# Moving the low-part subtractions of the mixing stages from GpSimd to VectorE

## The chip, the cores and the metric

One core of one Trainium2 chip runs the whole program. The metric is the device time of one execution in microseconds (us), given as the median of three runs. The engines are named as in the profile: PE is TensorE (PEld its weight loads), DVE is VectorE, ACT is ScalarE, POOL is GpSimd and SP issues transfers.

## The reference

Three layers follow each other. The first is windowed attention over q, k and v (4 batches, 8 heads, 576 tokens, 64 channels a head). The second is a mixture of four attention experts with two of them gated per token. The third is the one that the change touches; `x` is the result of the second layer, four batches of 576 tokens by 512 channels:

```python
theta = x @ w_theta
zr, zi = x * np.cos(theta), x * np.sin(theta)
y = np.einsum('ts,bsd->btd', w_tok_r, zr) + np.einsum('ts,bsd->btd', w_tok_i, zi)
u = x + y
return u + np.maximum(u @ w_ch, 0.0)
```

## The kernel before

**Split operands.** A matrix product in near-full precision is made of three products of a reduced format (`mm3`, L108 to L111): an operand is split into a high part (a cast by ACT) and a low part, the original minus the high part, and the kernel multiplies high by high, high by low and low by high. The helper `split` (L101) issues the ACT cast (L103) and then the subtraction (L106) on the engine that its last argument names. The subtraction needs the cast's result, so it waits for ACT.

**The stages at the end of the program.** The third layer is worked off by batch `b` and by half `dh` of the channels (256 columns each). `theta(b, dh)` (L649) goes through tiles of 128 tokens, 256 columns each; for every tile PE makes the angles and transposes x, ACT and DVE reduce the angle and take sine and cosine (L671 to L676), and DVE multiplies them with x (L679). That is the block z, 128x512, cosine half and sine half together. For the first three pairs (b, dh) the block is split straight away (L683). For the later ones two tiles are taken together by `sums_of` (L617): DVE makes four sums and differences of the blocks (L628, L629, L633, L637), and the blocks X, W, Y and V are split, each with an ACT cast and a subtraction. Tiles of the last 64 tokens of two batches are handled together (L687 to L694); their subtraction stands on GpSimd before and after the change.

**Mixing.** For the first three pairs `mix(b, dh)` (L697) multiplies the z blocks with the token weights; the later ones use `mix7` (L757), which makes a two by two block product with seven products instead of eight and needs X, W, Y and V for it. Both add the product to x2T on DVE (L717, L785), and four of the sums per `mix7` are also made on POOL (L791). The result, x plus y, is split in pieces of 128x288 as the input `cu` of the channel mixing (L718, L787). `channel(b)` (L833) multiplies with w_ch, DVE adds the rectified product (L843) and SP writes it out (L845).

**Work beside it.** `load_ch` (L878) turns the 64-bit channel weights into split parts in eight steps; each has a shift (L139) and a bit merge (L145) on DVE, an integer add on POOL (L147), a cast, and a subtraction on DVE (L153). `halves` (L720) makes combinations of the token weights for `mix7`: an add on POOL (L733), one on DVE (L734), four differences on DVE (L736 to L739) and splits.

**The order of the work.** `merge` (L50) interleaves the generators of a stage by cost numbers written by hand; the calls that matter here are L955 to L979. Then a scheduler orders each engine's instructions by that priority in its own simulated time, engine by engine, and places the semaphores. Every engine runs its instructions in that order, so an instruction that waits holds back everything behind it on its engine. `tc.issue_after(ins)` puts the instructions in its block that run on the engine of `ins` behind it. In `halves` the block at L732 stands under two of these: one names `d`, the DVE product of a z block (L679), and the other names `p`, the subtraction that `split` or `sums_of` returned for it:

```python
d, p = mark[((0, 1, 3), (1, 0, 0), (1, 0, 2), (1, 0, 3))[j]]
with tc.issue_after(p.ins), tc.issue_after(d.ins):
    nc.gpsimd.tensor_add(out=flat[:, 0], in0=f32(wkh[2 * j]), in1=f32(wkl[2 * j]))
    nc.vector.tensor_add(out=flat[:, 1], in0=f32(wkh[2 * j + 1]), in1=f32(wkl[2 * j + 1]))
```

Of the kernel before, what the change touches and what calls it, by code (L numbers as in the profile page):

```python
# [42 lines left out]
def f32(ap):  # L43
    return ap.bitcast(F32)
# [21 lines left out]
def kernel(ctx, tc, qT, kT, vw, consts, w_in, w_o, w_th, w_tk, w_ch, outT):  # L66
    nc = tc.nc
# [24 lines left out]
    def bank(shape, tag, name):  # L92
        return ps.tile(shape, F32, tag=tag, bufs=BANKS[tag], name=name)
# [7 lines left out]
    def split(dst_h, dst_l, src, eng_h, eng_l):  # L101
        if eng_h is nc.scalar:
            cast[0] = nc.scalar.copy(out=dst_h, in_=src)  # L103
        else:
            eng_h.tensor_copy(out=dst_h, in_=src)
        return eng_l.tensor_sub(out=dst_l, in0=src, in1=f32(dst_h))  # L106

    def mm3(out, wh, wl, xh, xl, first, last):  # L108
        nc.tensor.matmul(out, wh, xh, start=first, stop=False)  # L109
        nc.tensor.matmul(out, wh, xl, start=False, stop=False)  # L110
        nc.tensor.matmul(out, wl, xh, start=False, stop=last)  # L111
# [435 lines left out]
    Z, UH, XT, GT, mark, W4 = {}, {}, {}, {}, {}, 4 * P  # L547

    def hl_set(tags, name):
        t = [bp.tile([P, S], F32R, tag=tag, bufs=3 if tag in ("oh", "ol") else 1, name=f"{name}{i}")  # L550
             for i, tag in enumerate(tags)]
        return t[0::2], t[1::2]
# [27 lines left out]
    def load_o(n):  # L580
        while line and n:
            b, dh, i = line.pop(0)
            o = bp.tile([P, 4, P], F32R, tag=f"{'QK'[len(ring) % 4 // 2]}{'SA'[len(ring) % 4 // 2]}{len(ring) % 2}", name=f"or{b}{dh}{i}")
            nc.sync.dma_start(f32(o), od[b][:, :, i * P : i * P + P])
            ring.append(o)
            n -= 1
# [22 lines left out]
    def slot(tag, shape, name):  # L609
        pool, bufs = homes[tag]  # L610
        return pool.tile(shape, F32R, tag=tag, bufs=bufs, name=name)

    def operand(name):
        tag = free.pop(0)
        return tag, slot(tag, [P, 2, 2, 2, P], name)

    def sums_of(b, dh, i, ang):  # L617
        A11, A21, A12, A22 = (ang[:, :, q, k] for q in range(2) for k in range(2))
        if i == 1:
            Z[b, dh] = {}  # L620
        ops = Z[b, dh]
        n = f"{b}{dh}{i}"
        st = (rp if i == 1 else kp).tile([P, 2, 2, P], F32, tag="z", name=f"s{n}")
        s1, s2 = st[:, :, 0], st[:, :, 1]
        x = operand(f"X{n}")
        nc.scalar.copy(out=x[1][:, 0], in_=ang[:, :, :, 0])
        p = nc.gpsimd.tensor_sub(out=x[1][:, 1], in0=ang[:, :, :, 0], in1=f32(x[1][:, 0]))
        nc.vector.tensor_add(out=s1, in0=A21, in1=A22)  # L628
        nc.vector.tensor_sub(out=s2, in0=s1, in1=A11)  # L629
        w = operand(f"W{n}")  # L630
        nc.scalar.copy(out=w[1][:, 0], in_=st)
        nc.gpsimd.tensor_sub(out=w[1][:, 1], in0=st, in1=f32(w[1][:, 0]))
        nc.vector.tensor_sub(out=A21, in0=A11, in1=A21)  # L633
        y = operand(f"Y{n}")
        nc.scalar.copy(out=y[1][:, 0], in_=ang[:, :, :, 1])
        nc.gpsimd.tensor_sub(out=y[1][:, 1], in0=ang[:, :, :, 1], in1=f32(y[1][:, 0]))
        nc.vector.tensor_sub(out=A12, in0=A12, in1=s2)  # L637
        if i == 1:
            tag = free.pop(0)
            ops["V"] = tag, slot(tag, [P, 2, 4, P], f"V{n}")  # L640
        v = ops["V"][1]
        sl = slice(i - 1, i + 1)
        nc.scalar.copy(out=v[:, 0, sl], in_=A12)
        nc.vector.tensor_sub(out=v[:, 1, sl], in0=A12, in1=f32(v[:, 0, sl]))
        for k, t in zip("XWY", (x, w, y)):
            ops[k, i // 2] = t
        return p

    def theta(b, dh):  # L649
        x2 = x2T[b]  # L650
        dsl = slice(dh * HW, dh * HW + HW)
        for i in range(4 if b % 2 else 5):
            n = f"{b}{dh}{i}"
            if i < 4:
                tok = slice(i * P, i * P + P)
                o = ring[8 * b + 4 * dh + i]
                load_o(1)
                x32, ow = (lambda c: x2[:, c, tok]), [o[:, k] for k in range(4)]
            else:
                xt, xo = XT[0]  # L660
                x32, ow = (lambda c: xt[:, c]), [xo[:, k] for k in range(4)]
            th = bank([P, HW], "bs", f"th{n}")
            for c in range(2):
                mm3(th, ow[2 * c], ow[2 * c + 1], GT[c][0][:, dsl], GT[c][1][:, dsl], c == 0, c == 1)
            xk = bank([P, HW], "tb", f"xk{n}")
            for c in range(2):
                nc.tensor.transpose(xk[:, c * P : (c + 1) * P], x32(2 * dh + c), ident)
            if i % 2 == 0:
                ang = bp.tile([P, 2, 2, HW], F32, tag="bms", bufs=2, name=f"ang{n}")
            rn, sn = ang[:, i % 2, 0], ang[:, i % 2, 1]  # L670
            nc.scalar.activation(out=rn, in_=th, func=AF.Identity, bias=magic)  # L671
            nc.vector.scalar_tensor_tensor(out=rn, in0=rn, scalar=-MAGIC, in1=th,
                                           op0=ALU.add, op1=ALU.subtract)
            nc.scalar.activation(out=sn, in_=rn, func=AF.Sin, scale=-TWO_PI)
            nc.scalar.activation(out=rn, in_=rn, func=AF.Abs)
            nc.scalar.activation(out=rn, in_=rn, func=AF.Sin, bias=halfpi, scale=-TWO_PI)  # L676
            if i < 4:
                both = ang[:, i % 2]
                d = nc.vector.tensor_mul(out=both, in0=xk.unsqueeze(1).to_broadcast([P, 2, HW]), in1=both)  # L679
                if 2 * b + dh < 3:  # L680
                    zt = slot(first[8 * b + 4 * dh + i], [P, 2, 2, HW], f"z{n}")
                    Z[b, dh, i] = zt
                    mark[b, dh, i] = d, split(zt[:, :, 0], zt[:, :, 1], both, nc.scalar, nc.gpsimd)  # L683
                elif i % 2:
                    mark[b, dh, i] = d, sums_of(b, dh, i, ang.rearrange("p j q (k n) -> p j q k n", k=2))
            else:
                for k in range(2):  # L687
                    zt = kp.tile([P, 1, 2, HW], F32R, tag=f"zt{k}{dh}", name=f"z{n}{k}")
                    Z[b + k, dh, i] = zt
                    z = (rp, kp)[k].tile([P, HW], F32, tag="z", name=f"zf{n}{k}")  # L690
                    r = slice(64 * k, 64 * k + 64)
                    for q, tr in enumerate((rn, sn)):
                        nc.vector.tensor_mul(out=z[64 * q : 64 * q + 64], in0=xk[r], in1=tr[r])
                    split(zt[:, 0, 0], zt[:, 0, 1], z, nc.scalar, nc.gpsimd)  # L694
            yield 1.5

    def mix(b, dh):  # L697
        x2 = x2T[b]
        if dh == 0:
            UH[b] = hl_set(utags, f"cu{b}")  # L700
        uh, ul = UH[b]
        y = [bank([P, 288], tag, f"y{b}{dh}{k}") for k, tag in enumerate(("g", "g", "as", "ta"))]
        for c in range(9):
            zt = Z[b, dh, c // 2]
            q = c % 2 if c < 8 else 0
            for k in range(4):
                n, mm = divmod(k, 2)
                sl = slice(288 * n, 288 * n + 288)
                ms = slice(mm * P, mm * P + P)
                mm3(y[k], zt[:, q, 0, ms], zt[:, q, 1, ms], wkh[c][:, sl], wkl[c][:, sl],  # L710
                    c == 0, c == 8)
            yield 1.45
        for k in range(4):
            n, mm = divmod(k, 2)
            m = 2 * dh + mm
            sl = slice(288 * n, 288 * n + 288)
            nc.vector.tensor_add(out=x2[:, m, sl], in0=y[k], in1=x2[:, m, sl])  # L717
            split(uh[m][:, sl], ul[m][:, sl], x2[:, m, sl], nc.scalar, nc.gpsimd)  # L718

    def halves():  # L720
        f1 = rp.tile([P, 4, 288], F32, tag="x2b", name="t1")
# [35 lines left out]
    def mix7(b, dh):  # L757
        x2 = x2T[b]
        if dh == 0:
            UH[b] = hl_set(utags, f"cu{b}")  # L760
        uh, ul = UH[b]
# [22 lines left out]
        def add(m, sl, g, ready=False):  # L784
            nc.vector.tensor_add(out=x2[:, m, sl], in0=g, in1=x2[:, m, sl])  # L785
            if ready:
                split(uh[m][:, sl], ul[m][:, sl], x2[:, m, sl], nc.scalar, nc.gpsimd)  # L787

        def spread(u, *homes):
            for m, sl in homes:  # L790
# [3 lines left out]
        y = lambda k, tag: bank([P, 288], tag, f"y{k}{n}")  # L794
# [13 lines left out]
        g = y("d", "ta")  # L808
        yield from seven(g, lambda j: left(j, "W", 0), lambda j: TT[1, j], True, True)
        add(m1, s1, g)  # L810
        add(m2, s1, g)
        g = y("e", "g")
# [224 lines left out]
```

## Time and profile before

| what | us |
| --- | --- |
| median of three runs | 502.05 |
| lowest and highest | 500.07, 503.29 |
| the profiled execution, its time | 501.43 |
| the profiled execution, its span | 499.6 |

The span is the stretch between the first and the last instruction that the profile shows; the time has 1.8 us more around it. The profiled execution is 0.6 us below the median. All places in the trace are given in us from the start of the span: the third layer's mixing begins at about 300, `mix7` begins at about 374, the last channel mixing ends at about 496. "Idle before" in a group of instructions is the time that its engine stood still just before them, with what ended that wait.

### The profile page before, as it was taken

The page shows a single profiled execution, that of the slowest core. Times are in us where ns is not written, and L with a number is a line of the kernel's source. Part 1 is how long each engine was busy: PE and PEld are TensorE (multiplying, and loading weights), DVE is VectorE, ACT ScalarE, POOL GpSimd, SP SyncE. Part 2 cuts the span into 40 slices and gives each one's busy share as a digit, 9 for nine tenths or more (in the row PEclk, how much of TensorE's full clock was granted, in tenths as well). Part 3 has the DMA queues.
Part 4 walks back from the last instruction along what each step waited for, and adds up shares of the span by engine and source line. Part 5 has one row for each costly group of instructions (what it writes and reads, how often), then busy time and mean ns, then how long its engine had stood idle before and what let it go on. Part 6 is the DMA issues. An engine that isn't in the chain of part 4 may idle for free.

```text
span 499.6 us, 12071 instructions
## 1 busy us (share of the span) xinstructions
PE 475.9 (95%) x4128; PEld 446.2 (89%) x4128; DVE 381.6 (76%) x1283; ACT 342.2 (68%) x1054; POOL 319.3 (64%) x411
## 2 busy tenths in 40 slices
PE   7899899999999997999989999899999989999997
PEld 5689788999999897998878799899999989999997
DVE  6868989867779659877898969977668948893843
ACT  7948688867878756868787897876167717752620
POOL 6758789674776770323694556679558925891770
PEclk9999999999999999999999999999999999999999
DMA  8564253431316234112235953231362044202002
GB/s 272 182 227 134 67 179 108 139 100 49 125 60 198 78 97 147 33 38 92 88 120 168 349 176 144 71 78 43 100 175 65 23 143 131 65 22 96 2 0 96
DMA packets 45614, 55.92 MB, mean 112 GB/s; under 512 B 6641, under 2 KB 34289, under 8 KB 45553
## 3 DMA queue, kind: packets, MB, share of 16 engines
q1 hardware_dynamic: 44688, 52.46, 33.6%
q10 hardware_dynamic: 864, 2.69, 1.4%
q8 instruction: 33, 0.54, 0.4%
q14 instruction: 29, 0.23, 0.2%
HBM read 43.34 MB, written 11.80 MB: 110 GB/s over the span
## 4 chain that ended last, share of the span: by engine, by line
PE 52%; DVE 18%; ACT 15%; POOL 6%; issue 5%; DMA 3%; SPq 0%; DVEq 0%; ACTq 0%; POOLq 0%
PE as L297 3%; PE bpt L504 3%; ACT ams L313 2%; PE c L109 2%; PE c L110 2%; PE c L111 2%; PE apt L325 2%; PE qk L109 2%; PE bs L472 2%; PE qk L110 2%; PE ao L168 2%; PE qk L111 2%; PE bs L474 2%; PE o L522 2%; DMA wst<-in_dram 1%
## 5 line engine op out<-in xcount | busy, mean ns | idle before, releaser
L320 POOL TENSOR_TENSOR ams<-ams,arc 128x384 f32<-128x384 f32 x48 | 40.4, 845 | 34.4 <-DVE arc L319 14.3
L313 ACT ACTIVATE ams<-ams,anm 128x128 f32<-128x128 f32 x144 | 56.5, 396 | 4.0 <-DVE anm L305 2.9
L481 ACT ACTIVATE bms<-bms,bnm 64x64 f32<-64x64 f32 (+4 forms) x80 | 44.9, 562 | 13.1 <-DVE bnm L476 13.1
L297 PE MATMUL as<-kt,QD 128*128 128x128 f32 x288 | 41.2, 281 | 2.7 <-DVE anm L305 2.5
L297 PEld LDWEIGHTS as<-kt,QD 128*128 128x128 f32 x288 | 36.0, 192 | 6.2 <-DVE anm L305 2.9
L96 POOL TENSOR_SCALAR QD<-qt 64x576 f32<-64x576 f32 x24 | 30.6, 1274 | 11.7 <-DMA qt<-in_dram 4.6
L305 DVE CUSTOM_DVE_ANT_0 ams<-as,cst 128x128 f32<-128x128 f32 x144 | 34.1, 283 | 4.9 <-PE as L297 2.7
L476 DVE CUSTOM_DVE_ANT_0 bms<-bs,mb 64x64 f32<-64x64 f32 (+4 forms) x80 | 32.5, 422 | 5.4 <-PE bs L474 3.7
L106 POOL TENSOR_TENSOR cu<-x2T,cu 128x288 fp32r<-128x288 f32 x32 | 28.3, 901 | 9.9 <-ACT cu L103 9.8
L493 POOL TENSOR_SCALAR bpd<-bms,bsm,gw 128x64 f32<-128x64 f32 (+1 forms) x46 | 20.4, 445 | 20.2 <-DVE bsm L486 8.7
L109 PE MATMUL y<-wkh,z 128*128 128x288 f32 x108 | 32.1, 303 | 0.8 <-DVE x2T L717 0.8
L472 PE MATMUL bs<-KA,QS 128*128 128x288 f32 (+4 forms) x96 | 31.0, 331 | 1.1 <-DVE bnm L476 1.0
L110 PE MATMUL y<-wkl,z 128*128 128x288 f32 x108 | 31.9, 297 | 0.0
L679 DVE TENSOR_TENSOR ang<-xk,ang 128x512 f32<-128x512 f32 x32 | 21.6, 686 | 13.0 <-ACT ang L676 10.8
L111 PE MATMUL y<-wkh,z 128*128 128x288 f32 x108 | 30.9, 297 | 0.0
L671 ACT ACTIVATE ang<-th,magic 128x256 f32<-128x256 f32 x36 | 16.7, 470 | 18.8 <-PE th L111 17.7
L791 POOL TENSOR_TENSOR x2T<-x2T,u 128x288 f32<-128x288 f32 x20 | 16.9, 855 | 19.7 <-DVE u L802 18.1
L504 PE MATMUL bpt<-cst,bms 128*128 128x128 f32 x160 | 27.5, 276 | 1.5 <-ACT oh L103 1.5
L493 POOL TENSOR_SCALAR bms<-bms,bsm,gw 128x384 f32<-128x384 f32 (+3 forms) x38 | 24.7, 650 | 5.9 <-ACT wtuk L138 3.8
L474 PE MATMUL bs<-KL,QS 128*128 128x288 f32 (+4 forms) x96 | 28.4, 302 | 0.0
L313 ACT ACTIVATION_READ_ACCUMULATOR ams<-ams,anm 128x1 f32 x144 | 27.6, 192 | 0.0
L843 DVE SCALAR_TENSOR_TENSOR x2T<-c,x2T 128x288 f32<-128x288 f32 x32 | 13.8, 453 | 16.9 <-PE c L111 16.8
(337 smaller groups left out, 2051.7 us busy)
## 6 DMA issues: line engine op xcount, KB each, us to landing
vt<-in_dram SPq DMA_DIRECT2D x48, 192.0 KB, 2.9
or<-od SPq DMA_DIRECT2D x32, 256.0 KB, 3.3
kt<-in_dram SPq DMA_DIRECT2D x15, 320.0 KB, 3.1
qt<-in_dram SPq DMA_DIRECT2D x16, 288.0 KB, 3.6
out_dram<-x2T SPq DMA_DIRECT2D x32, 144.0 KB, 1.8
w64k<-in_dram SPq DMA_DIRECT2D x5, 576.0 KB, 4.2
od<-oh SPq DMA_DIRECT2D x8, 288.0 KB, 2.7
od<-ol SPq DMA_DIRECT2D x8, 288.0 KB, 2.8
```

Of the source, the lines that this page charges most:

```text
L109: nc.tensor.matmul(out, wh, xh, start=first, stop=False)
L110: nc.tensor.matmul(out, wh, xl, start=False, stop=False)
L111: nc.tensor.matmul(out, wl, xh, start=False, stop=last)
L297: nc.tensor.matmul(s[:, i, :], qd[:, blk], kt[:, 64 * blk : 64 * blk + 128], start=True, stop=True)
L305: nc.vector.tensor_tensor_reduce(out=ms[:, i, :], in0=s[:, i, :], in1=ma0 if (g == 0 and i == 0) else ma1, scale=-0.125, scalar=3.0e38, op ...
L313: nc.scalar.activation(out=ms[:, i, :], in_=ms[:, i, :], func=AF.Exp, bias=nm[:, i : i + 1], scale=-1.0, accum_out=sm[:, i, 0:1],)
L320: nc.gpsimd.tensor_mul(out=ms, in0=ms, in1=rc.unsqueeze(2).to_broadcast([P, 3, P]))
L472: nc.tensor.matmul(s[:, : z - a], qs[:, q0 : q0 + P], ka[:, a:z], start=True, stop=False)
L474: nc.tensor.matmul(s[:, : z - a], qs[:, q0 : q0 + P], KL[e][:, a:z], start=False, stop=True)
L481: ex = nc.scalar.activation(out=ms[:m, :w], in_=ms[:m, :w], func=AF.Exp, bias=nm[:m, ci : ci + 1], scale=-1.0, accum_out=ss[:m, i, 0:1])
L493: eng.tensor_scalar(out=dst, in0=src, scalar1=sm[:m, i : i + 1], scalar2=gw[:m, t, 2 * ep + i : 2 * ep + i + 1], op0=ALU.mult, op1=ALU.mult)
L504: nc.tensor.transpose(pt[:, jj, i, :], pn[:, i, P * j : P * j + P], ident)
```

## The change

Six subtractions get another engine: the low parts of X, W and Y in `sums_of`, those of the z blocks that `theta` splits directly, and those of the channel mixing's input in `mix` and `mix7`. Nothing else is edited. No operand, tile, transfer or matmul differs.

```diff
         x = operand(f"X{n}")
         nc.scalar.copy(out=x[1][:, 0], in_=ang[:, :, :, 0])
-        p = nc.gpsimd.tensor_sub(out=x[1][:, 1], in0=ang[:, :, :, 0], in1=f32(x[1][:, 0]))
+        p = nc.vector.tensor_sub(out=x[1][:, 1], in0=ang[:, :, :, 0], in1=f32(x[1][:, 0]))
         nc.vector.tensor_add(out=s1, in0=A21, in1=A22)
         nc.vector.tensor_sub(out=s2, in0=s1, in1=A11)
         w = operand(f"W{n}")
         nc.scalar.copy(out=w[1][:, 0], in_=st)
-        nc.gpsimd.tensor_sub(out=w[1][:, 1], in0=st, in1=f32(w[1][:, 0]))
+        nc.vector.tensor_sub(out=w[1][:, 1], in0=st, in1=f32(w[1][:, 0]))
         nc.vector.tensor_sub(out=A21, in0=A11, in1=A21)
         y = operand(f"Y{n}")
         nc.scalar.copy(out=y[1][:, 0], in_=ang[:, :, :, 1])
-        nc.gpsimd.tensor_sub(out=y[1][:, 1], in0=ang[:, :, :, 1], in1=f32(y[1][:, 0]))
+        nc.vector.tensor_sub(out=y[1][:, 1], in0=ang[:, :, :, 1], in1=f32(y[1][:, 0]))
         nc.vector.tensor_sub(out=A12, in0=A12, in1=s2)
...
-                    mark[b, dh, i] = d, split(zt[:, :, 0], zt[:, :, 1], both, nc.scalar, nc.gpsimd)
+                    mark[b, dh, i] = d, split(zt[:, :, 0], zt[:, :, 1], both, nc.scalar, nc.vector)
...
-            split(uh[m][:, sl], ul[m][:, sl], x2[:, m, sl], nc.scalar, nc.gpsimd)
+            split(uh[m][:, sl], ul[m][:, sl], x2[:, m, sl], nc.scalar, nc.vector)
...
             if ready:
-                split(uh[m][:, sl], ul[m][:, sl], x2[:, m, sl], nc.scalar, nc.gpsimd)
+                split(uh[m][:, sl], ul[m][:, sl], x2[:, m, sl], nc.scalar, nc.vector)
```

## Rows read from the trace of the kernel before

**Rows 1.** The page, part 1: busy time of each engine, whole span.

```profile
PE 475.9 (95%) x4128; PEld 446.2 (89%) x4128; DVE 381.6 (76%) x1283; ACT 342.2 (68%) x1054; POOL 319.3 (64%) x411
```

**Rows 2.** Stretches: length, busy us of each engine, granted clock, DMA share, GB/s.

```profile
300.00:402.00 102.00, 97.20 (x731) 94.51 (x730) 83.27 (x151) 68.49 (x170) 76.45 (x70) 1.00 0.29 85
402.00:486.00 84.00, 84.00 (x649) 84.00 (x648) 56.86 (x104) 41.05 (x96) 51.82 (x51) 1.00 0.23 68
```

**Rows 3.** Waits of PE from 300 to 500: us, times, longest.

```profile
PE c L109 <- DVE zf L693: 1.3, 1, 1.3
PE th L109 <- DVE ang L672: 1.2, 1, 1.2
PE y L109 <- DVE x2T L717: 0.8, 2, 0.6
PE yh L109 <- DVE x2T L785: 0.7, 1, 0.7
```

**Rows 4.** POOL groups from 300 to 402: busy, mean ns, idle before.

```profile
L106 POOL TENSOR_TENSOR z<-ang,z 128x512 fp32r<-128x512 f32 x12 | 16.0, 1342 | 3.8 <-ACT z L103 3.8
L106 POOL TENSOR_TENSOR cu<-x2T,cu 128x288 fp32r<-128x288 f32 x16 | 14.4, 921 | 1.8 <-ACT cu L103 1.8
...
L627 POOL TENSOR_TENSOR X<-ang,X 128x512 fp32r<-128x512 f32 x4 | 5.6, 1392 | 0.6 <-ACT X L626 0.6
L636 POOL TENSOR_TENSOR Y<-ang,Y 128x512 fp32r<-128x512 f32 x4 | 5.6, 1389 | 0.0
L632 POOL TENSOR_TENSOR W<-s,W 128x512 fp32r<-128x512 f32 x4 | 5.5, 1387 | 2.0 <-ACT W L631 2.0
```

**Rows 5.** DVE operations by line: shortest, median and longest ns.

```profile
L679 DVE TENSOR_TENSOR ang<-xk,ang x20: 673/692/692, 300.0 to 392.2; 128x512 f32<-128x512 f32 x20
L633 DVE TENSOR_TENSOR ang<-ang x10: 410/1024/1514, 370.8 to 473.9; 128x256 f32<-128x256 f32 x10
L843 DVE SCALAR_TENSOR_TENSOR x2T<-c,x2T x32: 443/457/460, 349.5 to 496.4; 128x288 f32<-128x288 f32 x32
L139 DVE TENSOR_SCALAR wtuc<-wtuc x8: 281/656/1380, 300.8 to 321.7; 128x256 uint32<-128x256 uint32 x8
```

**Rows 6.** DVE groups from 300 to 402: busy, mean ns, idle before.

```profile
L139 DVE TENSOR_SCALAR wtuc<-wtuc 128x256 uint32<-128x256 uint32 x8 | 5.5, 692 | 0.1
...
L629 DVE TENSOR_TENSOR s<-s,ang 128x256 f32<-128x256 f32 x4 | 5.0, 1249 | 0.0
...
L736 DVE TENSOR_TENSOR t<-f 128x288 f32<-128x288 f32 x4 | 4.5, 1122 | 4.8 <-POOL f L733 4.8
L644 DVE TENSOR_TENSOR V<-ang,V 128x256 fp32r<-128x256 f32 x4 | 3.8, 943 | 0.7 <-ACT V L643 0.7
L637 DVE TENSOR_TENSOR ang<-ang,s 128x256 f32<-128x256 f32 x4 | 3.5, 863 | 0.0
L628 DVE TENSOR_TENSOR s<-ang 128x256 f32<-128x256 f32 x4 | 3.2, 803 | 0.1
...
L633 DVE TENSOR_TENSOR ang<-ang 128x256 f32<-128x256 f32 x4 | 2.9, 719 | 0.0
```

**Rows 7.** Timeline of DVE and POOL, 318 to 322: start, us.

```profile
318.89 1.19 DVE L139 TENSOR_SCALAR wtuc<-wtuc 128x256 uint32<-128x256 uint32 x1
320.11 1.38 DVE L145 SCALAR_TENSOR_TENSOR wtuc<-w64c,wtuc 128x256 uint32<-128x256 uint32 x1
321.42 0.41 DVE L672 SCALAR_TENSOR_TENSOR ang<-ang,th 128x256 f32<-128x256 f32 x1
...
318.59 2.62 POOL L106 TENSOR_TENSOR z<-ang,z 128x512 fp32r<-128x512 f32 x2 [1.04 <-ACT z L103]
```

**Rows 8.** Timeline of DVE and POOL, 398 to 402: start, us.

```profile
398.58 1.53 DVE L644 TENSOR_TENSOR V<-ang,V 128x256 fp32r<-128x256 f32 x1
...
398.54 1.30 POOL L636 TENSOR_TENSOR Y<-ang,Y 128x512 fp32r<-128x512 f32 x1
...
400.66 0.80 POOL L106 TENSOR_TENSOR cu<-x2T,cu 128x288 fp32r<-128x288 f32 x1
```

## The prediction

> **What bounds the kernel now.** I read the busy shares first: PE is busy for 95% of the span [rows 1]. Then I cut the mixing stages into stretches. The changed instructions run from about 302 us on, so nothing earlier should differ. Between 402 and 486 PE is busy for 84.0 of 84.0 us; between 300 and 402 it is busy for 97.2 of 102, so 4.8 us of PE time stand idle there, at a granted clock of 1.00 throughout, which is the 2.4 GHz level [rows 2]. That is the frame of the whole prediction. The change adds and removes no matmul, so in these stages it can give back those 4.8 us and no more; and what it does after 402 is free as long as PE's inputs come in time.
>
> The third view is PE's waits. The four large ones, 4.0 us together, all end with a DVE instruction, none with POOL [rows 3]. In that stretch DVE is busy 83.3 of 102 us and POOL 76.5 [rows 2]. So the question is whether DVE reaches those four instructions earlier or later when it takes over POOL's subtractions.
>
> **What moves.** In 300 to 402 POOL makes 12 z subtractions, 4 each for X, W and Y, and 16 for the channel input: 16.0 + 5.6 + 5.5 + 5.6 + 14.4 = 47.1 us [rows 4]. The trace has no DVE subtraction of 128x512 with both inputs in SBUF. Nearest is the product of the same width with one input in PSUM, 0.68 us; for 128x288 it is the rectified add, 0.45 us [rows 5]. I take these two: 24 x 0.68 + 16 x 0.45 = 16.3 + 7.2 = 23.5 us more on DVE. The lower end is 0.41 us for each of the 40, the shortest two-input row of half the width [rows 5]: 16.4 us. The upper end is that they are stretched as the present DVE work with two SBUF inputs is, which takes 0.72 to 1.25 us on average where 0.41 is its shortest [rows 5, 6]: twice the price, 47 us, which is also what POOL needs. I stay by 23.5, since most of POOL's reading moves away with them.
>
> **What DVE gets back.** The same DVE line takes 0.41 us at best and 1.51 at worst [rows 5], though its shape never changes. Two places show why. At 318.89 a shift and a bit merge take 1.19 and 1.38 us while POOL makes two z subtractions of 2.62 us together, and the end of the second one and the end of the merge nearly coincide [rows 7]. At 398.58 the subtraction of V takes 1.53 us beside POOL's subtraction for Y [rows 8]. I read this as DVE being held while POOL reads.
>
> The Trainium skill, in "SBUF — State Buffer", section "Who interferes with whom", says that VectorE and GpSimd share one pair of SBUF ports as an exclusive lock: a VectorE operation with two SBUF inputs and a GpSimd operation that reads SBUF block each other for the whole instruction. The rows just named agree. The same rule speaks against the change as well, since the new subtractions have two SBUF inputs and will be held by what stays on POOL; a sum by the rule is the lower relief worked out next.
>
> At their shortest the five lines of `sums_of` would take 20 x 0.41 = 8.2 us instead of 5.0 + 3.8 + 3.5 + 3.2 + 2.9 = 18.4: 10.2 back. The shift at 0.28 gives 5.5 - 2.2 = 3.3, the first difference of `halves` at 0.45 gives 4.5 - 1.8 = 2.7 [rows 5, 6]. Together 16.2 us if nothing on POOL held DVE any more. But only 47.1 of POOL's 76.5 us move [rows 2, 4], that is 62%; by that share 10.0 us come back. Other stretched lines of the weight loading and of `halves` add something that I leave uncounted. So DVE's load in the stretch changes by 23.5 - 16.2 = +7.3 to 23.5 - 10.0 = +13.5 us, to 90.6 to 96.8 of 102. It is not DVE work that is saved, but POOL work, and POOL is not what PE waits for.
>
> **The four waits, one by one.** (a) At 320, 1.2 us: the reduction of the angle stood behind the shift and the merge, 2.57 us; alone they take 0.28 and about 0.41, and the two z subtractions now in the same queue 1.36, together 2.05. DVE arrives 0.5 us sooner: -0.5 [rows 3, 5, 7]. (b) At 399.6, 1.3 us: V's subtraction shrinks from 1.53 to 0.41 us, but Y's 0.68 and one channel subtraction of 0.45 come into the queue, 1.13 against 1.12: 0 [rows 3, 5, 8]. (c) The 0.8 us behind the adds at L717, mostly at 342, where the long first difference of `halves` stands in front: 1.12 on average against 0.45 + 0.68 for a z subtraction in front of it gives nothing on average, up to 0.7 if the z subtraction is placed elsewhere: -0.35 [rows 3, 5, 6]. (d) 0.7 us behind the add at L785, in the middle of `sums_of`: one set costs 18.4 / 4 = 4.6 us now and 5 x 0.41 + 3 x 0.68 = 4.1 afterwards; half of the wait goes: -0.35 [rows 3, 5, 6]. Sum: -1.2 us.
>
> **What I cost at nothing.** After 402 DVE is busy 56.9 of 84 us [rows 2]; a net addition in proportion to the first stretch stays under 13.5 us, so there is room, and PE has no gap to lose. If that cover goes, each us by which DVE is late is a us on PE. The moved subtractions issue no transfer and pass no transfer on SP's or POOL's queue. The edge in `halves` changes sides: `p` is now a DVE instruction, so L734 is put behind it on DVE and L733 on POOL loses it. The DVE waits for L733 of 4.8 us [rows 6] can shrink by that; nothing on PE is late for `halves` in rows 3, so I take 0, with -0.8 as the lower end and +0.8 as the upper, the wait at L717 gone or doubled.
>
> **Sum.** The profiled execution took 501.43 us; -1.2 gives 500.2. It lies 0.6 below the median of 502.05, so against the runs shown the forecast is 500.9. A measurement can tell about 1%, 5 us, from no change.
>
> **Rivals.** First, all of PE's idle time goes: the scheduler places the new subtractions behind the urgent instructions, and DVE's stretching vanishes. Then -4.8: 497.2. For it speaks that every large wait ends with DVE and that several stand behind stretched instructions; against it that DVE's total rises even with all the relief.
>
> Second, on the other side: DVE inherits POOL's waits for ACT. Each moved subtraction needs a cast first. POOL stood idle for casts for 3.8 + 1.8 + 0.6 + 2.0 = 8.2 us in the stretch [rows 4], with nothing urgent behind it. On DVE, the reductions of angles and the adds that free PSUM banks are queued behind such a wait, and PE waits for these. Price: 13.5 more work plus 8.2 of waits is 21.7, against 18.7 us of DVE idle time now [rows 2]. That idle time is itself partly waits; if two thirds of it, 12.5, can be filled, 9.2 us are left over, and if about two thirds of these reach PE, +6: 508. It decides from the point at which the additions pass those 12.5 us.
>
> Third, the change doesn't do what it seems to, because the stretch has another cause than POOL's reading. Then the relief is nothing, DVE has 83.3 + 23.5 = 106.8 us of work in a stretch of 102, and 4.8 us over plus the waits of 3 to 4 that DVE keeps make about +8: 510. Against it stand the coincidences in rows 7 and 8.
>
> A rule that gives no change: the Trainium skill says in "Perfetto Trace Analysis", section "Optimizing Scalar/DVE Operations", that moving work between GpSimd and VectorE might not help because they share a port. Under it the time would stay near 502, inside the forecast's case; the trace of before can't test it.
>
> **Chances.** Forecast, within 3 us of 500.9: 0.57. All gaps gone: 0.17. DVE inherits the waits: 0.21. No relief: 0.05. The likeliest case is the predicted time. For 8 in 10 I take 496.5 at the low end, just past the first rival, and 508 at the high end, the second rival's time. Faster by over 1% (under 497.0) is half of the first rival, 0.08, and 0.05 for an order of instructions that also closes the small gaps that rows 3 leave out: 0.13. Slower by over 1% (over 507.1) is two thirds of the second rival, 0.14, most of the third, 0.04, and 0.03 for an order that opens new gaps: 0.21. The rest is no change: 0.66.
>
> **What would show it.** Right: DVE's busy time between 300 and 402 rises to 85 to 97 us while POOL's falls below 35; the five lines of `sums_of` come near 0.41 to 0.6 us; new 128x512 subtractions take about 0.7; PE's idle time there stays at 3 to 5 us; 402 to 486 stays full. Wrong: a new PE wait that ends with a DVE subtraction standing behind an ACT cast (second rival), lines of `sums_of` still near 1 us (third), or PE idle under 1 us (first).

## The result, and the profile after

The changed kernel takes 495.13 us (median of 5 runs, 494.83 to 498.5) against 502.05 before: a ratio of 0.988, 95% interval 0.984 to 0.992. On a second occasion it gave 495.86 and 0.987 (0.984 to 0.991). So it is faster by 1.2%, 6.9 us, where 1.2 us were forecast; the time lies 1.4 us below the range. The profiled execution's span went from 499.6 to 493.3 us, 6.3 less.

The busy shares of the page's part 1 (after), to be read against [rows 1]:

```profile
PE 474.1 (96%) x4128; PEld 447.5 (91%) x4128; DVE 390.7 (79%) x1357; ACT 341.6 (69%) x1054; POOL 235.8 (48%) x337
```

DVE has 74 instructions and 9 us more, POOL 74 and 84 us fewer. The same two stretches as in [rows 2], in the kernel after; the columns are length, then busy us and count of PE, PEld, DVE, ACT and POOL, granted clock, DMA share and GB/s:

```profile
300.00:402.00 102.00, 101.04 (x781) 100.63 (x780) 90.53 (x194) 68.25 (x172) 33.17 (x33) 1.00 0.30 90
402.00:486.00 84.00, 84.00 (x650) 84.00 (x649) 62.36 (x140) 41.74 (x97) 14.10 (x16) 1.00 0.24 70
```

The second stretch was full and stays full: the whole gain lies in the first. There 781 matmuls fall into the window instead of 731. At the average rate of the full stretch, 84.0 / 650 = 0.129 us each, these 50 are worth an estimated 6.5 us, which is the gain. PE's busy column would explain only 101.0 - 97.2 = 3.8 us of it. PEld's column tells it nearly right: 100.6 - 94.5 = 6.1.

PE's waits from 300 to 500 after; none of the four in [rows 3] is left, and one on ACT is new:

```profile
PE y L109 <- ACT ttKL L103: 0.7, 1, 0.7
PE x L109 <- ACT oh L103: 0.2, 1, 0.2
```

DVE's groups of instructions from 300 to 402 after (busy, mean ns, idle before), the moved ones, those of [rows 6], and L734, the add of `halves` on DVE:

```profile
L106 DVE TENSOR_TENSOR z<-ang,z 128x512 fp32r<-128x512 f32 x12 | 9.0, 760 | 0.8 <-ACT z L103 0.7
L106 DVE TENSOR_TENSOR cu<-x2T,cu 128x288 fp32r<-128x288 f32 x16 | 8.5, 543 | 0.0
...
L734 DVE TENSOR_TENSOR f<-wkh,wkl 128x576 f32<-128x576 f32 x4 | 4.8, 1192 | 1.5 <-POOL tw L106 1.5
...
L632 DVE TENSOR_TENSOR W<-s,W 128x512 fp32r<-128x512 f32 x4 | 3.3, 820 | 0.0
L627 DVE TENSOR_TENSOR X<-ang,X 128x512 fp32r<-128x512 f32 x4 | 3.2, 802 | 0.0
L636 DVE TENSOR_TENSOR Y<-ang,Y 128x512 fp32r<-128x512 f32 x4 | 2.7, 685 | 0.0
L736 DVE TENSOR_TENSOR t<-f 128x288 f32<-128x288 f32 x4 | 2.7, 665 | 0.8 <-POOL f L733 0.6 <-ACT ang L675 0.2
L139 DVE TENSOR_SCALAR wtuc<-wtuc 128x256 uint32<-128x256 uint32 x8 | 2.4, 314 | 0.0
...
L628 DVE TENSOR_TENSOR s<-ang 128x256 f32<-128x256 f32 x4 | 1.7, 415 | 0.0
L637 DVE TENSOR_TENSOR ang<-ang,s 128x256 f32<-128x256 f32 x4 | 1.7, 415 | 0.0
L629 DVE TENSOR_TENSOR s<-s,ang 128x256 f32<-128x256 f32 x4 | 1.7, 415 | 0.0
L633 DVE TENSOR_TENSOR ang<-ang 128x256 f32<-128x256 f32 x4 | 1.7, 414 | 0.0
...
L644 DVE TENSOR_TENSOR V<-ang,V 128x256 fp32r<-128x256 f32 x4 | 1.6, 412 | 0.0
```

The moved work costs 9.0 + 8.5 + 3.3 + 3.2 + 2.7 = 26.7 us. The five lines of `sums_of` fall from 18.4 to 8.4 us, to within 0.01 us of their shortest each; the shift from 5.5 to 2.4. The last column is as telling: the idle time before z and the channel input is 0.8 (0.7 of it for the cast) and 0.0, where POOL stood 3.8 and 1.8 [rows 4].

One line went the other way: L734 takes 4.8 us where it took 3.0 in the kernel before. At 336.74 it runs for 1.97 us, against 0.75 at its shortest, beside the add L733, which reads on POOL as it did. The cast that PE waits for in the 0.7 us row above follows a few DVE instructions behind it, so the readers that stayed on POOL seem to cost something still.

Last, the place at 320. PE of the kernel before, then of the kernel after; `x2` counts two transposes in one row:

```profile
320.26 0.38 PE L667 MATMUL xk<-cst,x2T 128*128 128x128 f32 x2
321.88 0.39 PE L109 MATMUL th<-wot,xo 128*128 128x256 f32 x1 [1.24 <-DVE ang L672]
```

```profile
320.65 0.38 PE L667 MATMUL xk<-cst,x2T 128*128 128x128 f32 x2
320.79 0.37 PE L109 MATMUL th<-wot,xo 128*128 128x256 f32 x1
```

From start to start it is 1.62 us before and 0.14 after: 1.48 lost, though the row notes a wait of 1.24. The matmuls overlap, and each is drawn 0.3 to 0.4 us long while one starts every 0.13 us, so every gap is covered in part by the tail of the one before. Counted like this, from start to start less the usual step, the places of [rows 3] held 1.48 us at 320, 0.77 and 0.58 at 342 and 354 (both L717), 0.83 at 387 and 1.42 at 400: 5.1 us, where the rows note 4.0. DVE at that place, after:

```profile
319.02 0.41 DVE L672 SCALAR_TENSOR_TENSOR ang<-ang,th 128x256 f32<-128x256 f32 x1
...
319.81 0.69 DVE L106 TENSOR_TENSOR z<-ang,z 128x512 fp32r<-128x512 f32 x1
320.42 0.28 DVE L139 TENSOR_SCALAR wtuc<-wtuc 128x256 uint32<-128x256 uint32 x1
```

The reduction that PE waited for now runs ahead of the z subtraction and of the shift that stood in front of it [rows 7].

### The profile page after: what moved, and what is told of

It reads as the page before. It is cut to its first block, busy times and chain, and to the rows that moved or that the text cites. A ratio compares the mean times of both kernels' runs of the same rounds, so it can differ in the third digit from the quotient of the medians.

```text
span 493.3 us, 12028 instructions
## 1 busy us (share of the span) xinstructions
PE 474.1 (96%) x4128; PEld 447.5 (91%) x4128; DVE 390.7 (79%) x1357; ACT 341.6 (69%) x1054; POOL 235.8 (48%) x337
## 4 chain that ended last, share of the span: by engine, by line
PE 66%; DVE 12%; ACT 9%; DMA 5%; issue 3%; POOL 3%; SPq 1%; ACTq 0%; DVEq 0%; POOLq 0%
PE as L297 4%; PE c L111 3%; PE c L109 3%; PE c L110 3%; PE bpt L504 3%; PE apt L325 2%; PE qk L109 2%; PE qk L110 2%; PE qk L111 2%; PE ao L168 2%; PE bs L472 2%; DMA qt<-in_dram 2%; PE o L522 2%; PE bs L474 2%; ACT bms L481 2%
## 5 line engine op out<-in xcount | busy, mean ns | idle before, releaser
L791 POOL TENSOR_TENSOR x2T<-x2T,u 128x288 f32<-128x288 f32 x20 | 17.8, 902 | 82.1 <-ACT u L798 50.5
L103 ACT CAST cu<-x2T 128x288 fp32r<-128x288 f32 x32 | 13.3, 429 | 18.9 <-DVE x2T L785 9.8
```

## The experiments

Two theories stood after the result. A: the gain comes from durations; POOL's subtractions, by reading SBUF, had stretched DVE's instructions with two SBUF inputs and the shift. B: the gain comes from the order; with other engines named, the scheduler wrote another sequence, in which urgent instructions stand earlier, the add L733 among them, which lost its edge to `p`. Every kernel below also has an order of its own.

**One part each.** Only X, W and Y on DVE (the three lines of the diff in `sums_of`):

```diff
-        nc.gpsimd.tensor_sub(out=w[1][:, 1], in0=st, in1=f32(w[1][:, 0]))
+        nc.vector.tensor_sub(out=w[1][:, 1], in0=st, in1=f32(w[1][:, 0]))
...
```

> Only the three subtractions in sums_of (X, W, Y) are made by DVE. Theory A (what counts is that POOL's reading no longer stretches DVE): the five DVE lines of sums_of fall from 0.7 to 1.25 us to under 0.55, PE's gaps after 375 (about 2.9 us in start-to-start terms) go and those at 320, 342 and 354 (about 3.4 us) stay: 2 to 3.5 us faster than before, ratio about 0.994. Theory B (what counts is the order the scheduler makes, not the durations): the place of the gain does not follow the place of the move; gaps before 366 change as well.

Measured 500.48 us, ratio 0.996 (0.994 to 0.998). The larger of PE's waits from 300 to 500 in this kernel:

```profile
PE c L109 <- DVE zf L693: 1.5, 1, 1.5
PE th L109 <- DVE ang L672: 1.2, 1, 1.2
PE y L109 <- DVE x2T L717: 0.8, 2, 0.6
```

The wait on L785, in the midst of `sums_of`, is gone. The waits on L672 and L717, where only z subtractions lie, stand as before to the tenth; PE's sequence is the same as before up to 377, so these rows alone don't tell A from B. Two things I had expected did not come: the wait before the channel mixing at 400 stays, and of the five lines of `sums_of`, 12.2 us together in the first stretch instead of 18.4, two stay above 0.55 us, L628 at 0.75 and L633 at 0.72.

Only the z blocks on DVE:

```diff
-                    mark[b, dh, i] = d, split(zt[:, :, 0], zt[:, :, 1], both, nc.scalar, nc.gpsimd)
+                    mark[b, dh, i] = d, split(zt[:, :, 0], zt[:, :, 1], both, nc.scalar, nc.vector)
```

> Only the subtractions of the z blocks that theta splits directly are made by DVE. Theory A: the shift L139 and the merge L145 fall to about 0.3 and 0.45 us, the gaps at 320, 342 and 354 go, those after 375 stay: 2.5 to 3.5 us faster, ratio about 0.994. Theory B: the same place would gain from the order alone, and the lines of sums_of, still stretched, would not matter for the gaps after 375: 4 us faster or more.

Measured 499.75 us, ratio 0.994 (0.991 to 0.997). Its larger waits:

```profile
PE y L109 <- DVE x2T L717: 1.3, 1, 1.3
PE yh L109 <- DVE x2T L785: 1.0, 1, 1.0
PE c L109 <- DVE zf L693: 0.7, 1, 0.7
```

The mirror image: the shift and the merge fall to 0.31 and 0.41 us and the wait at 320 is gone, the one in `sums_of` is there again. One miss: the wait at 342 grew from 0.6 to 1.3 instead of going. In front of that add DVE now makes a z subtraction of 0.68 us, and L734 before it takes 1.98 us. Apart from the waits at 342 and 400, the gain appears where the work was moved, as A says.

Only the channel mixing's input on DVE:

```diff
-                split(uh[m][:, sl], ul[m][:, sl], x2[:, m, sl], nc.scalar, nc.gpsimd)
+                split(uh[m][:, sl], ul[m][:, sl], x2[:, m, sl], nc.scalar, nc.vector)
...
```

> Only the channel mixing's input (32 subtractions of 128x288) is made by DVE. Theory A (POOL's reading stretches DVE): z, X, W and Y stay on POOL and go on stretching DVE, DVE gets 7.2 us of work more between 300 and 402, and the relief is that of 14.4 us of POOL work only: between 1 us faster and 2 us slower than before, ratio 0.998 to 1.004. The sum of the three parts alone would then be close to the whole: e1 -0.43%, e2 -0.62%, this part near -0.1%. Theory B (the schedule's order): no relation between the sum of the parts and the whole; 3 us faster or slower is as likely.

Measured 505.32 us, ratio 1.007 (1.004 to 1.009): slower, beyond what A allowed it. Its stretches, to be read against [rows 2]:

```profile
300.00:402.00 102.00, 97.13 (x742) 94.39 (x742) 85.53 (x162) 70.14 (x174) 64.02 (x53) 1.00 0.30 88
402.00:486.00 84.00, 82.38 (x625) 81.05 (x624) 63.21 (x117) 40.72 (x95) 40.22 (x36) 1.00 0.23 68
```

In the first stretch nothing is lost. In the second, which was full, 24 matmuls fewer fall into the window, an estimated 3.1 us, which is the whole loss. DVE and then PE at the longest new wait there, at 446:

```profile
444.20 1.06 DVE L106 TENSOR_TENSOR cu<-x2T,cu 128x288 fp32r<-128x288 f32 x1
445.19 1.50 DVE L637 TENSOR_TENSOR ang<-ang,s 128x256 f32<-128x256 f32 x1
446.61 0.44 DVE L785 TENSOR_TENSOR x2T<-yf,x2T 128x288 f32<-128x288 f32 x1
446.98 1.27 DVE L679 TENSOR_TENSOR ang<-xk,ang 128x512 f32<-128x512 f32 x2
```

```profile
447.71 0.40 PE L109 MATMUL c<-cu,wch 128*128 128x288 f32 x1 [1.18 <-DVE ang L679]
```

The moved subtraction takes 1.06 us instead of 0.45, beside POOL's add L791, and L637 behind it 1.50 instead of 0.41, beside W and Y on POOL; the product that PE waits for comes late by that. (At 398 a moved subtraction takes even 1.52 us and PE waits 1.2 for it, but the kernel before had a wait of 1.3 at that place.) A part that goes alone puts one more two-input instruction on DVE into POOL's way. The parts do not add up: -0.43, -0.62 and +0.65% make -0.40, the whole is -1.2.

**The whole without the channel part.** z, X, W and Y on DVE, the channel input on POOL, beside the whole change again.

> z, X, W and Y on DVE, the channel mixing's input left on POOL: the whole change less the part that costs 0.65% when it is made alone. If the parts simply added up, this would be the best version, 1.05% to 1.8% faster than before and 0 to 3 us faster than the whole change. Theory A with its limit (PE has hardly a gap left to give back once z, X, W and Y have moved, and the channel part has room on a DVE that is no longer stretched): 495 to 499, not faster than the whole change; the gap at about 400, which stayed with X, W, Y alone and half stayed with z alone, tells whether the channel part is needed to close it.

> The changed kernel once more, on the same chip and with the same runs of before as the kernel that leaves the channel part on POOL, so that the two can be compared: 494 to 497 us, ratio 0.985 to 0.990.

Measured 497.11 us, 0.991 (0.987 to 0.994), against 495.86, 0.987 (0.984 to 0.991), for the whole. Its two larger waits:

```profile
PE y L109 <- DVE x2T L717: 1.3, 1, 1.3
PE c L109 <- DVE zf L693: 0.9, 1, 0.9
```

z, X, W and Y carry most of the gain, and theirs add up within the error (-0.43 and -0.62 against -0.95%). The channel part, harmful alone, costs nothing once the rest has left POOL. The two intervals overlap, so whether it helps is not settled; the wait at 396 that remains here is absent in the whole.

**POOL's reading put back.** The changed kernel; POOL adds the two halves of each operand into a scratch tile:

```diff
         nc.vector.tensor_sub(out=w[1][:, 1], in0=st, in1=f32(w[1][:, 0]))
+        again(f32(w[1][:, 0]), f32(w[1][:, 1]))
...
+        nc.gpsimd.tensor_sub(out=o, in0=a, in1=b)
```

(The scratch instruction is a subtraction; it takes 0.90 us for 128x288 and 1.36 to 1.56 for 128x512 on average, the moved ones 0.92 and 1.34 to 1.39 [rows 4].)

> The changed kernel, and POOL also adds the high and the low part of every operand whose low part DVE now makes, into a scratch tile that nothing reads: 74 more POOL instructions of the shapes that were moved. Theory A: DVE's lines with two SBUF inputs are stretched again to 0.6 us and more, DVE runs out of time between 300 and 402, and the kernel is 4 to 10 us slower than the changed one, 500 to 505. Theory B: POOL has the time, nothing waits for the scratch: within 2 us of the changed kernel, 493 to 497.

Measured 530.3 us, ratio 1.053 (1.050 to 1.057): 35 us above the changed kernel. A has the direction, and its 4 to 10 us are far too small. Groups of DVE from 300 to 520 in this kernel (busy, mean ns; lines are moved down by the insertions, L659 is V's subtraction):

```profile
L106 DVE TENSOR_TENSOR cu<-x2T,cu 128x288 fp32r<-128x288 f32 x32 | 21.1, 668 | 1.2 <-ACT cu L103 0.9
...
L106 DVE TENSOR_TENSOR z<-ang,z 128x512 fp32r<-128x512 f32 x12 | 13.0, 1091 | 0.7 <-ACT z L103 0.7
...
L659 DVE TENSOR_TENSOR V<-ang,V 128x256 fp32r<-128x256 f32 x10 | 11.2, 1116 | 0.0
L650 DVE TENSOR_TENSOR Y<-ang,Y 128x512 fp32r<-128x512 f32 x10 | 11.0, 1104 | 0.0
```

Each moved subtraction is itself held now: 128x512 takes 0.9 to 1.1 us on average, V 1.1 instead of 0.41. And PE, over the same stretch as above:

```profile
300.00:402.00 102.00, 90.37 (x656) 87.71 (x651) 94.31 (x160) 60.61 (x153) 63.57 (x54) 0.95 0.28 85
```

DVE is busy for 94 of 102 us and still does less than in the changed kernel, 160 instructions against 194; 656 matmuls fall into the window, 125 fewer. The granted clock of 0.95 of the 2.4 GHz level stands beside a PE that idles; it explains 5% of this stretch at most. No wait of PE, DVE or ACT in this kernel ends with a scratch instruction, so it isn't that operands come free later. I had counted the stretch of the old lines and not that of the moved ones. The moved work's price leaves its forecast here: 64.5 us for these 74 subtractions against 43 at 0.68 and 0.45, 1.5 times, half of the way to the upper bound of twice the price.

**POOL busy without reading.** The kernel before; POOL fills the moved low parts with zeros:

```diff
-        nc.gpsimd.tensor_sub(out=w[1][:, 1], in0=st, in1=f32(w[1][:, 0]))
+        nc.gpsimd.memset(f32(w[1][:, 1]), 0.0)
...
```

> The kernel before, where POOL fills the moved low parts with zeros instead of subtracting: the low parts of z, X, W, Y and of the channel mixing's input are left out of the result. POOL writes as much but reads nothing there, and DVE gets no work added. Theory A in the form that POOL's reading is what holds DVE: DVE's lines fall to their shortest though POOL is still busy, PE's gaps after 302 go, 493 to 497 us. If instead POOL's being busy at all, its writing included, holds DVE, the lines of sums_of stay above 0.7 us and the time at 498 to 502.

Measured 495.07 us, ratio 0.986 (0.984 to 0.988): what the change gives, with no work added to DVE. So the 26.7 us that the change adds to DVE cost nothing measurable; the reading on POOL was the cost. Timeline of POOL and DVE at 367 in this kernel:

```profile
367.20 0.53 POOL L627 MEMSET X<- 128x512 f32 x1 [1.22 <-PE y L111]
367.67 0.53 POOL L636 MEMSET Y<- 128x512 f32 x1
```

```profile
366.94 0.43 DVE L629 TENSOR_TENSOR s<-s,ang 128x256 f32<-128x256 f32 x1
367.29 0.42 DVE L633 TENSOR_TENSOR ang<-ang 128x256 f32<-128x256 f32 x1
367.62 0.42 DVE L637 TENSOR_TENSOR ang<-ang,s 128x256 f32<-128x256 f32 x1
```

Two fills run beside three two-input instructions and hold none of them. It is so throughout this kernel: of the lines L628, L629, L633 and L637, the 18 instructions that overlap fills and nothing else on POOL take 0.41 to 0.43 us each, and the two that take 0.9 and 1.0 us lie beside POOL's remaining add (L791, here L794). The shift, with one SBUF input, behaves otherwise (POOL, then DVE):

```profile
316.60 0.74 POOL L106 TENSOR_TENSOR z<-zf,z 128x256 fp32r<-128x256 f32 x1
317.29 0.99 POOL L684 MEMSET z<- 128x512 f32 x2
```

```profile
316.73 1.69 DVE L139 TENSOR_SCALAR wtuc<-wtuc 128x256 uint32<-128x256 uint32 x1
```

It begins beside a subtraction and lasts until the two fills behind that are over, 1.69 us instead of 0.29; at 309.59 another does the same, 1.31 us. Two shifts that began before the fill beside them kept 0.30 and 0.29. One caveat: a fill is shorter than a subtraction, 0.53 against 1.34 us, and waits for no cast, so this kernel takes away POOL time as well as reading; the instructions beside fills alone are what separates them.

**The lost edge.** The kernel before without the edge to `p`, and the changed kernel with it:

```diff
-            with tc.issue_after(p.ins), tc.issue_after(d.ins):
+            with tc.issue_after(d.ins):
```

> The kernel before with one thing taken over from the change: in halves the adds L733 and L734 no longer stand behind p, so L733 can go early on POOL. Theory A: no gain, within 1.5 us of before, since POOL still reads as much. Theory B, in the form that the lost edge made the better order: 3 to 6 us faster than before.

```diff
-                nc.gpsimd.tensor_add(out=flat[:, 0], in0=f32(wkh[2 * j]), in1=f32(wkl[2 * j]))
+                r = nc.gpsimd.tensor_add(out=flat[:, 0], in0=f32(wkh[2 * j]), in1=f32(wkl[2 * j]))
+                tc.add_manual_dep(r.ins, p.ins.name, mybir.DependencyInfo(mybir.DependencyClass.NoSync, mybir.DependencyReason.DATA), reason="as before")
```

> The changed kernel, with the order edge put back that the change lost: the adds L733 on POOL stand behind p again. Theory A: the same as the changed kernel, 494 to 497 us, with the five lines of sums_of at 0.41 us. Theory B, the lost edge made the order better: 498 us or more.

Measured 505.72 us, ratio 1.006 (1.003 to 1.008), and 496.5 us, ratio 0.987 (0.984 to 0.991). Losing the edge alone makes the old kernel slower, outside what either theory expected, and having it back changes nothing in the new one. B in this form is out. Why the old kernel gets slower is not shown: its order differs, but DVE is stretched more as well (L734 takes 1.38 us on average in the first stretch instead of 0.76), and PE's waits behind L717 grow from 0.8 to 2.6.

**More of the same.** The changed kernel with the low parts of the last tokens, of `halves` and of `halves_end` on DVE too:

```diff
-            split(h, l, flat[:, 1], nc.scalar, nc.gpsimd)
+            split(h, l, flat[:, 1], nc.scalar, nc.vector)
...
```

> The changed kernel, and three more low parts go from POOL to DVE: those of the last 64 tokens (8 of 128x256) and those of halves and halves_end (4 of 128x576, 4 of 128x288), about 8 x 0.41 + 4 x 0.75 + 4 x 0.45 = 8 us of DVE work. Theory A: PE has only about 1 us of larger gaps left after 302, so at best 1 us faster than the changed kernel, and at worst 3 us slower where DVE runs out of time before 350: 493.5 to 498.

Measured 496.53 us, ratio 0.989 (0.986 to 0.991): no further gain. PE has little to give: in the changed kernel the weight loads leave 1.4 us of the first stretch.

**Taken together.** Five kernels have the five lines of `sums_of` at 8.3 to 9.7 us in the first stretch (after, the edge put back, more moved, zeros instead of subtractions, the channel part left): all lie at 495 to 497 us. Three have them at 15.2 to 18.4 (before, the edge gone, the channel part alone): 502 to 506. The two halves lie between, each with one part relieved: X, W, Y alone 12.2 us with the shift still at 5.5, z alone 18.8 with the shift at 2.4. The order differs in all of them. That is theory A. A difference in the order may add to it: the kernel without the edge, where more than the order changed, was slower by about half a percent. Not tried: the old sequence of instructions with the new engines.

## Why the prediction was wrong

- **The frame failed.** "It can give back those 4.8 us and no more" took PE's idle time from its busy column in [rows 2]. The same row says 731 matmuls; at 0.129 us 102 us hold 788, so 57 were missing, an estimated 7.4 us. That estimate borrows the mix of the second stretch, and the kernel with the fills got 797 into the first; it is no ceiling. PEld's column says it too: 102 - 94.5 = 7.5. The Trainium skill, in "Trainium Kernel Development and Optimization", section "Performance Expectations", calls the matmuls' busy time a bad measure of how close a kernel is to its roofline, because they are pipelined, and the weight loads' a good one. Here the trace agrees: PEld's idle time fell by 6.1 us and the span by 6.3. The first rival, all gaps gone, was the case that came; its 497.2 would have been 502.05 less 7.4, about 494.7.
- **The four waits, one by one, failed as a sum.** -1.2 us were forecast. From start to start (a) gave back 1.48 where 0.5 were forecast, (b) 1.42 where 0 were, (d) 0.83 where 0.35 were. Only (c) came out about as forecast: of its 0.77 and 0.58 the new wait on ACT's cast at the same place leaves 0.95. Together that is -4.1; the rest of the 6.3 us, 2.2, lies in smaller gaps that rows 3 leave out. For (a) and (d) I put the new subtractions in front of the instruction that PE waits for. At (a) neither stands there: one z subtraction is made at 315.77 and the other at 319.81, behind the reduction at 319.02. A subtraction makes an operand for later, while the reduction frees banks now. At (d), 381.23 in the kernel after, only that of X stands in front of the add; W's and Y's come later. For (b), X, W and Y alone left the wait at 400, and the whole closed it; what closed it was not followed instruction by instruction.
- **DVE's load came out right in part by luck**: +7.3 to +13.5 forecast, 83.27 to 90.53 measured, +7.3. POOL fell to 33.2, below 35. But the moved work cost 26.7 us, not 23.5 (the price of 0.68 holds as a median, the means are 0.69 to 0.82), so the relief was 26.7 - 7.3 = 19.4, where 10.0 to 16.2 were reckoned. The 62% share was too little: the five lines gave back 10.0 of their 10.2, the shift 3.1 of 3.3, and lines left uncounted the rest. The two misses cancel at the lower end.
- **The cause of the stretch was right.** The rule that the prediction weighed from the Trainium skill, "SBUF — State Buffer", section "Who interferes with whom", agrees with the runs on both sides: in the old kernel, where L633 took up to 1.51 us, and in the kernel that reads twice, where the moved V takes 1.12 us on average instead of 0.41. The third rival is out, and so is the case of no change: the move gave 1.2%.
- **The second rival did not come.** DVE waits for casts before the moved subtractions were 0.7 us for z and none for the channel input in that stretch, not 8.2: DVE has other work in between. The nearest to it is the channel part alone, where PE does wait behind a DVE subtraction, through the stretch and not through the cast.
- **The edge, costed at nothing,** cost nothing in the changed kernel.

What stays open: why the single parts leave or enlarge the waits at 342 and 400 was read from one profile each, and not taken further; nor why the old kernel without the edge is slower.

## What to carry to other kernels

Here an operation on POOL that reads SBUF had two prices, its own time and what it held up on DVE. Before such a move, compare the same DVE line's shortest and mean duration, and count the difference as DVE's relief; the kernel gains of it what PE's waits give back (19.4 us of relief, 6.9 of gain). Try all such readers of a stage together, for a part can cost more than nothing. And take PE's idle time from its weight loads, or from the count of matmuls against a full stretch of a like mix, not from its busy share.

## What the runs showed of the hardware that was not expected

Two-input reads on both engines cost far more than the 4 to 10 us that were expected: 74 extra POOL instructions, 88.8 us in sum on an engine that had room for them, made the kernel 35 us longer. A POOL fill did not hold a two-input DVE instruction (0.41 to 0.43 us beside fills alone), but it did hold a one-input shift that had begun beside a POOL instruction in front of the fill: 1.69 and 1.31 us instead of 0.29.
